# The bias of a spatial gating unit: from a matmul into PSUM to a product on POOL and an add on DVE

## The chip, the cores and the metric

The kernel runs on one core of a Trainium2 chip. The metric is the device time of one execution in microseconds (us); a profile of one execution goes with it. The engines are named as in the profile: PE (matmul), PEld (its weight loads), DVE (vector), ACT (scalar), POOL (GpSimd) and SP (which only issues DMAs here).

## The reference

Grouped attention of 16 query heads over 4 key and value heads, followed by a gated feed-forward unit whose gate mixes the tokens of a sequence. The types are FP32 outside.

```python
# batch 8, 16 q heads, 4 kv heads, seq 384, head_dim 64; d_model 1024, d_ff 1024
k = np.repeat(k, 4, axis=1); v = np.repeat(v, 4, axis=1)
scores = q @ k.transpose(0, 1, 3, 2) / sqrt(64)
attn = softmax(scores)
x = (attn @ v).transpose(0, 2, 1, 3).reshape(8, 384, 1024)

h = np.maximum(x @ w_in, 0.0)
u, v = h[..., :512], h[..., 512:]
v_n = (v - mean(v)) / np.sqrt(var(v) + 1e-06)          # over the 512 features
v_s = einsum('ts,bsd->btd', w_spatial, v_n) + b_spatial[None, :, None]
out = (u * v_s) @ w_out                                # 8 x 384 x 1024
```

The bias belongs to a token t and is the same for all features.

## The kernel before

All matmuls are FP16 with FP32 sums in PSUM. The instruction order of each engine is the order in which the program issues, written out by hand; an engine runs its own list in order and waits on semaphores for the others.

**The outer loop** (L552) counts steps n from 0 to 149, 18 for each batch b (NU = 18). A step issues, in this order:
- what is due by the table `todo`: loads, casts of k, q and v to FP16 on POOL, DMA transposes on SP (`k_turn`, `q_turn`, `x_turn`);
- `scores` (L243): for one group of heads and one key tile a pair of score matmuls into `sc` (L252) and an exp on ACT into `aT` (L259). From batch 1 on, every even step issues two of these and every odd step none;
- `weigh` (L261): 12 matmuls of `aT` against v into the PSUM tile `av` (L266), then on DVE a reciprocal (L276) and the scaling into `x16` (L278, called x in the profile). `av` has one buffer. With rem = n mod 18, a weighing comes at every rem that leaves 0 or 1 when divided by 3, and none where it leaves 2;
- transposes on PE by the table `turns` (batch 0, batch 1 and the end of the last batch);
- `run_fill`: a share of the gated unit of the batch whose attention is finished.

**The gated unit** is a Python generator, `gated_unit` (L306), that yields after each matmul the number of its columns, and `run_fill` (L542) takes from it until the step's share is used up. For a batch it holds 24 matmuls for v (three token tiles of eight, L314, with relu, statistics and their aggregate on DVE, L324 to L327), 32 for u (L336, relu on ACT, L344), the normalisation of v (ACT L346 and L347, DVE `nmr` L349, POOL `vn` L354), 16 for the gating, and 24 for the projection (L384, with copies to `osb` on DVE and ACT in turn, L393, and the stores on SP). Its columns are counted in `COLS`, 43008, and a step takes COLS/18. The unit of batch b starts at n = 18(b+1) + 2, and that of batch 0 earlier, at n = 13, with smaller shares up to n = 20.

**The gating** (L364 to L377) makes, for each of four feature tiles m, one PSUM tile `psp` of 128 features by 384 tokens: first a matmul of the constant `ones_b` against `bias_b` (L366), then three of `vn` against the transposed spatial weights (L369). `ones_b` has ones in rows 0 and 32; `bias_b` holds in row 0 the bias in FP16 and in row 32 what FP16 leaves of it, in the order of the token tiles, so that the matmul adds the bias with nearly FP32 precision. DVE multiplies `psp` by `uT` into `gT` (L377). `prep_spatial` (L408) fills `bias_b` on POOL at step 20, from `b32`, which is loaded at step 13.

Fill tiles share one PSUM tag, `ck`, with three buffers: `pv`, `pu`, `psp` and `po`, and the transposes.

Of the kernel before, what the change touches and what calls it, by code (L numbers as in the profile page):

```python
# [9 lines left out]
FP32 = mybir.dt.float32  # L10
FP16 = mybir.dt.float16
AF = mybir.ActivationFunctionType
ALU = mybir.AluOpType
# [4 lines left out]
def kernel(  # L18
# [28 lines left out]
    scale = D ** -0.5  # L47
    VW = D + 2
    NU = 18
# [235 lines left out]
    def x_tile(b):  # L285
        if b not in xts:
            xts[b] = att.tile([P, NT, NB, P], FP16, name=f"xt_{b}", tag="xt")
        return xts[b]
# [13 lines left out]
        )  # L302

    def gated_unit(b):  # L306
        xt = x_tile(b)
        last = b == B - 1
        mv = small.tile([P, NT, 2], FP32, name=f"mv_{b}", tag="mv")
        v_r, v_n = [], []  # L310
        for st in range(NT):
            pv = ps_ck.tile([P, 512], FP32, name=f"pv_{b}_{st}", tag="ck")
            for kt in range(NB):
                nc.tensor.matmul(  # L314
                    pv,
                    xt[:, st, kt],
                    w_in16[:, kt, DH:DFF],
                    start=(kt == 0),
                    stop=(kt == NB - 1),
                )  # L320
                if kt < NB - 1:
                    yield 512
            vr = moe.tile([P, DH], FP32, name=f"vr_{b}_{st}", tag="vr", bufs=4)
            nc.vector.tensor_scalar(vr, pv, 0.0, None, op0=ALU.max)  # L324
            stats = small.tile([P, 6], FP32, name=f"stats_{b}_{st}", tag="stats")
            nc.vector.bn_stats(stats, vr)  # L326
            nc.vector.bn_aggr(mv[:, st, :], stats)  # L327
            v_r.append(vr)
            yield 512
        rstd = small.tile([P, NT], FP32, name=f"rstd_{b}", tag="rstd")  # L330
        nmr = small.tile([P, NT], FP32, name=f"nmr_{b}", tag="nmr")
        uT = moe.tile([P, NM, S], FP16, name=f"uT_{b}", tag="uT")
        for m in range(NM):
            pu = ps_ck.tile([P, 512], FP32, name=f"pu_{b}_{m}", tag="ck")
            for kt in range(NB):
                nc.tensor.matmul(  # L336
                    pu[:, 0:S].rearrange("p (t s) -> p t s", t=NT),
                    w_in16[:, kt, m * P : (m + 1) * P],
                    xt[:, :, kt],
                    start=(kt == 0),  # L340
                    stop=(kt == NB - 1),
                )
                yield S
            nc.scalar.activation(uT[:, m, :], pu[:, 0:S], AF.Relu)  # L344
            if m == 0:
                nc.scalar.activation(rstd, mv[:, :, 1], AF.Ln, bias=eps_t)  # L346
                nc.scalar.activation(rstd, rstd, AF.Exp, scale=-0.5)  # L347
            if m == 1:
                nc.vector.scalar_tensor_tensor(  # L349
                    nmr, mv[:, :, 0], -1.0, rstd, op0=ALU.mult, op1=ALU.mult  # L350
                )
                for st in range(NT):
                    vn = moe.tile([P, DH], FP16, name=f"vn_{b}_{st}", tag="vn", bufs=6)
                    nc.gpsimd.tensor_scalar(  # L354
                        vn,
                        v_r[st],
                        rstd[:, st : st + 1],
                        nmr[:, st : st + 1],
                        op0=ALU.mult,
                        op1=ALU.add,  # L360
                    )
                    v_n.append(vn)
        gT = moe.tile([P, NM, S], FP16, name=f"gT_{b}", tag="gT")
        for m in range(NM):  # L364
            psp = ps_ck.tile([P, 512], FP32, name=f"psp_{b}_{m}", tag="ck")
            nc.tensor.matmul(psp[:, 0:S], ones_b, bias_b, start=True, stop=False)  # L366
            yield S
            for st in range(NT):
                nc.tensor.matmul(  # L369
                    psp[:, 0:S],  # L370
                    v_n[st][:, m * P : (m + 1) * P],
                    wsT16[:, st, :],
                    start=False,
                    stop=(st == NT - 1),
                )
                yield S
            nc.vector.tensor_tensor(gT[:, m, :], psp[:, 0:S], uT[:, m, :], ALU.mult)  # L377
        rows = out[b].rearrange("(p t) d -> p t d", t=NT)
        for tt in range(NT):
            osb = ops.tile([P, DM], FP32, name=f"osb_{b}_{tt}", tag="osb")  # L380
            for half in range(2):
                po = ps_ck.tile([P, 512], FP32, name=f"po_{b}_{tt}_{half}", tag="ck")
                for m in range(NM):
                    nc.tensor.matmul(  # L384
                        po,
                        gT[:, m, tt * P : (tt + 1) * P],
                        w_out16[:, m, half * 512 : (half + 1) * 512],
                        start=(m == 0),
                        stop=(m == NM - 1),
                    )  # L390
                    yield 512
                cols = slice(half * 512, (half + 1) * 512)
                (nc.scalar.copy if half else nc.vector.tensor_copy)(osb[:, cols], po)  # L393
                if last:
                    nc.sync.dma_start(rows[:, tt, cols], osb[:, cols])
            if not last:
                nc.sync.dma_start(rows[:, tt, :], osb)

    HV = NB * 512
    COLS = NT * HV + NM * NB * S + NM * (NT + 1) * S + NT * 2 * NM * 512  # L400


    b32 = cst.tile([1, S], FP32, name="b32")

    def load_b():
        nc.sync.dma_start(b32, moe_b_spatial.rearrange("(a s) -> a s", a=1))

    def prep_spatial():  # L408
        lo32 = cst.tile([1, S], FP32, name="lo32")
        bp = b32.rearrange("a (p t) -> a t p", t=NT)  # L410
        hi = bias_b[0:1, :].rearrange("a (t p) -> a t p", t=NT)
        nc.gpsimd.tensor_copy(hi, bp)
        nc.gpsimd.tensor_tensor(lo32.rearrange("a (t p) -> a t p", t=NT), bp, hi, ALU.subtract)
        nc.gpsimd.tensor_copy(bias_b[32:33, :], lo32)

    def load_ws():
        t = cst.tile([P, NT, S], FP32, name="ws32")
# [117 lines left out]
            elif m > 3:  # L535
                at(s0 + 3 * m + 5, x_turn, b, 2, 4 * (m - 4), 4 * (m - 3))

    fill = []
    owed = 0.0
    total = NU * B  # L540

    def run_fill(cols):  # L542
        nonlocal owed
        owed = owed + cols if fill else 0.0
        while fill and owed > 0:
            try:
                owed -= next(fill[0])
            except StopIteration:
                fill.pop(0)

    early = 0
    for n in range(total + 6):  # L552
        for f, args in todo.pop(n, []):
            f(*args)
        if n + 1 < NU:
            scores(n + 1)
        elif n >= NU and n % 2 == 0 and n < total:
            scores(n)
            scores(n + 1)
        for hh in range(2):  # L560
            b, r = divmod(n - 3 - hh, NU)
# [4 lines left out]
        if n == 13:  # L566
            fill.append(gated_unit(0))
        if n >= 2 * NU + 2 and (n - 2) % NU == 0 and (n - 2) // NU <= B:
            fill.append(gated_unit((n - 2) // NU - 1))
# [7 lines left out]
    for g in fill:  # L577
        for _ in g:
            pass
    assert not todo and not turns  # L580
# [1 line left out]
_INS = ['q', 'k', 'v', 'moe_w_in', 'moe_w_spatial', 'moe_b_spatial', 'moe_w_out']  # L582
# [26 lines left out]
```

## Time and profile before

| | |
|---|---|
| time, median of 3 runs | 257.72 us (257.62 to 259.6) |
| profiled execution | 256.98 us, of which the span is 254.9 us |
| granted TensorE clock | 0.999 |
| PE busy | 244.5 us (96%) |
| ACT busy | 169.0 us (66%) |
| DVE busy | 140.6 us (55%) |
| POOL busy | 73.8 us (29%) |
| HBM read, written | 25.76 MB, 12.58 MB |

The span runs from the first to the last instruction. Busy time is the union over an engine's instructions; the mean of one instruction can be longer than its share of that, since matmuls overlap. A row of the groups gives line, engine, operation, output from inputs, shapes and count, then busy us and mean ns of one, and the idle time before them with what ended most of it. A row of the timeline gives start and length in us, then engine and operation, with neighbours of one kind merged (x2, x3).

### The profile page before, as it was taken

The numbers are of one execution on the slowest core, as the hardware profiler recorded it, in microseconds if no ns is written. First come the engines' busy times: TensorE is split into PE (matmuls) and PEld (weight loads), VectorE is DVE, ScalarE is ACT, GpSimd is POOL, SyncE is SP. The second block draws the span as 40 slices with busy tenths as digits, with TensorE's granted clock in tenths as the row PEclk, the third lists the DMA queues.
The fourth block names the chain that finished last, engine by engine and source line by source line (L and its number), as shares of the span: only waits on it lengthen the run. The fifth ranks groups of instructions, "written<-read, shape, count | busy, mean of one in ns | idle before, by whom it ended". The sixth has DMA issues, their size and how long they took to land.

```text
span 254.9 us, 5897 instructions
## 1 busy us (share of the span) xinstructions
PE 244.5 (96%) x2400; PEld 126.6 (50%) x2400; DVE 140.6 (55%) x368; ACT 169.0 (66%) x219; POOL 73.8 (29%) x116
## 2 busy tenths in 40 slices
PE   6899899899999999999999999999999999999994
PEld 6565444544455445544455445544455445545551
DVE  2568775364736456454736456454736456465542
ACT  3897566767686767767686767767686767761221
POOL 2446699652032500343032500342030000300210
PEclk9999999999999999999999999999999999999999
DMA  7999899999269971999359991999277364026006
GB/s 184 326 357 346 299 372 326 212 323 299 64 117 302 232 247 25 202 302 281 95 111 293 257 239 30 165 324 346 39 88 152 102 188 41 3 44 247 0 4 245
DMA packets 78828, 49.86 MB, mean 196 GB/s; under 512 B 48081, under 2 KB 72658, under 8 KB 78802
## 3 DMA queue, kind: packets, MB, share of 16 engines
q1 hardware_dynamic: 77762, 49.23, 74.1%
q8 instruction: 19, 0.31, 0.5%
q10 hardware_dynamic: 1040, 0.26, 0.5%
q14 instruction: 7, 0.06, 0.1%
HBM read 25.76 MB, written 12.58 MB: 150 GB/s over the span
## 4 chain that ended last, share of the span: by engine, by line
PE 88%; ACT 3%; DVE 3%; DMA 2%; issue 1%; POOL 1%; SPq 0%; DVEq 0%; POOLq 0%
PE pu L336 16%; PE av L266 16%; PE po L384 15%; PE pv L314 14%; PE sc L252 14%; PE psp L369 6%; PE warm L453 3%; DMA xt<-x 2%; ACT aT L259 2%; PE psp L366 2%; PE qps L217 1%; ACT osb L393 1%; DVE x L278 1%; DVE gT L377 1%; POOL vn L354 1%
## 5 line engine op out<-in xcount | busy, mean ns | idle before, releaser
L259 ACT ACTIVATE aT<-sc 128x1024 f16<-128x1024 f32 x144 | 139.6, 1022 | 56.9 <-PE sc L252 56.5
L266 PEld LDWEIGHTS <-aT 128*128 128x128 f16 x1152 | 44.0, 97 | 30.5 <-issue 6.2
L276 DVE RECIPROCAL r<-av 128x4 f32<-128x4 f32 x96 | 17.0, 177 | 67.2 <-PE av L266 67.2
L266 PE MATMUL av<-v,aT 128*128 128x65 f16 x1152 | 52.3, 194 | 1.1 <-DVE x L278 0.8
L354 POOL TENSOR_SCALAR vn<-vr,rstd,nmr 128x512 f16<-128x512 f32 x24 | 18.2, 774 | 113.4 <-DVE nmr L349 91.7
L336 PE MATMUL pu<-xt,w_in 128*128 128x384 f16 x256 | 47.8, 326 | 0.6 <-ACT uT L344 0.6
L384 PE MATMUL po<-w_out,gT 128*128 128x512 f16 x192 | 47.8, 379 | 0.4 <-ACT osb L393 0.3
L314 PE MATMUL pv<-w_in,xt 128*128 128x512 f16 x192 | 47.2, 379 | 0.6 <-DMA xt<-x 0.4
L252 PE MATMUL sc<-qT,kT 64*128 64x512 f16 x288 | 45.0, 382 | 1.0 <-DVE qT L224 0.6
L278 DVE TENSOR_TENSOR x<-av,r 128x256 f16<-128x256 f32 x96 | 40.7, 424 | 3.3
L336 PEld LDWEIGHTS <-w_in 128*128 128x128 f16 x256 | 23.1, 98 | 15.9 <-issue 3.4
L189 POOL CAST q<-q 128x768 f16<-128x768 f32 (+1 forms) x36 | 25.5, 740 | 18.3 <-DMA q<-in_q_dram 13.6
L314 PEld LDWEIGHTS <-xt 128*128 128x128 f16 x192 | 16.7, 97 | 18.5 <-DMA xt<-x 2.4
L384 PEld LDWEIGHTS <-gT 128*128 128x128 f16 x192 | 16.7, 97 | 16.1 <-DVE gT L377 1.7
L377 DVE TENSOR_TENSOR gT<-psp,uT 128x384 f16<-128x384 f32 x32 | 17.7, 556 | 10.5 <-PE psp L369 9.8
L369 PE MATMUL psp<-wsT,vn 128*128 128x384 f16 x96 | 22.3, 326 | 0.7 <-POOL vn L354 0.7
L252 PEld LDWEIGHTS <-kT 64*128 64x128 f16 x288 | 9.1, 94 | 27.0 <-issue 25.2
L324 DVE TENSOR_SCALAR vr<-pv 128x512 f32<-128x512 f32 x24 | 16.6, 691 | 10.2 <-PE pv L314 9.7
L393 ACT COPY osb<-po 128x512 f32<-128x512 f32 x24 | 14.1, 589 | 12.1 <-PE po L384 12.1
L344 ACT ACTIVATE uT<-pu 128x384 f16<-128x384 f32 x32 | 15.6, 492 | 9.3 <-PE pu L336 9.3
L393 DVE COPY osb<-po 128x512 f32<-128x512 f32 x24 | 16.5, 687 | 6.1 <-PE po L384 6.0
L326 DVE BATCH_NORM_STATS2 stats<-vr 128x6 f32<-128x512 f32 x24 | 16.7, 694 | 0.8
(48 smaller groups left out, 113.5 us busy)
## 6 DMA issues: line engine op xcount, KB each, us to landing
q<-in_q_dram SPq DMA_DIRECT2D x14, 768.0 KB, 7.5
out_dram<-osb SPq DMA_DIRECT2D x21, 512.0 KB, 3.6
wi<-in_moe_w_in_dram SPq DMA_DIRECT2D x4, 1024.0 KB, 8.8
v<-in_v_dram SPq DMA_DIRECT2D x8, 384.0 KB, 8.6
k<-in_k_dram SPq DMA_DIRECT2D x7, 384.0 KB, 4.6
wo<-in_moe_w_out_dram SPq DMA_DIRECT2D x2, 1024.0 KB, 5.9
out_dram<-osb SPq DMA_DIRECT2D x6, 256.0 KB, 2.1
q<-in_q_dram SPq DMA_DIRECT2D x2, 512.0 KB, 7.2
```

Of the source, the lines that this page charges most:

```text
L189: f(q16s[b, j][:, lo:hi, :, hh, :], src[:, hh, lo:hi])
L252: nc.tensor.matmul(sc[:, hh], kTs[b][half, j, t * P : (t + 1) * P], qTs[b, j][half, qt], start=True, stop=True,)
L259: nc.scalar.activation(aTs[b, m][:, t], sc, AF.Exp, scale=scale)
L266: nc.tensor.matmul(av[:, i, :], aTs[b, m][:, t, hh, i * P : (i + 1) * P], v1[b % 2][:, 2 * j + hh, t, 0 : D + 1], start=(t == 0), stop=(t ...
L278: nc.vector.tensor_tensor(x16s[b][:, qt, blk : blk + 2].rearrange("p k (i d) -> p (k i) d", i=2), av[:, :, 0:D], r.to_broadcast([P, G, D]) ...
L314: nc.tensor.matmul(pv, xt[:, st, kt], w_in16[:, kt, DH:DFF], start=(kt == 0), stop=(kt == NB - 1),)
L336: nc.tensor.matmul(pu[:, 0:S].rearrange("p (t s) -> p t s", t=NT), w_in16[:, kt, m * P : (m + 1) * P], xt[:, :, kt], start=(kt == 0), stop ...
L354: nc.gpsimd.tensor_scalar(vn, v_r[st], rstd[:, st : st + 1], nmr[:, st : st + 1], op0=ALU.mult, op1=ALU.add,)
L369: nc.tensor.matmul(psp[:, 0:S], v_n[st][:, m * P : (m + 1) * P], wsT16[:, st, :], start=False, stop=(st == NT - 1),)
L377: nc.vector.tensor_tensor(gT[:, m, :], psp[:, 0:S], uT[:, m, :], ALU.mult)
L384: nc.tensor.matmul(po, gT[:, m, tt * P : (tt + 1) * P], w_out16[:, m, half * 512 : (half + 1) * 512], start=(m == 0), stop=(m == NM - 1),)
L393: (nc.scalar.copy if half else nc.vector.tensor_copy)(osb[:, cols], po)
```

## The change

The matmul against `ones_b` goes, and with it `ones_b` and the two-row form of `bias_b`. `bias_b` becomes a 128-partition FP32 tile; the DMA that loads `b32` broadcasts the bias to all partitions, and `prep_spatial` is one POOL copy that sorts it into the order of the token tiles.

The output of a gate is now written as u*psp + u*bias. POOL makes the second term, `ub`, one FP32 product of 128 x 384 for each m (`biases`, issued after the four blocks of u). DVE makes the first term into an FP32 tile `g` and adds `ub` into `gT`: two DVE operations for each m where there was one.

The generator is cut into pieces that one endless `stream` puts in order. In it, v of the next batch's first token tile stands between the gating and the projection of a batch, so a batch's own part starts with its second token tile. The normalisation is issued after the first block of u instead of partly after the second. `COLS` loses the bias matmuls (41472), the small shares of the start last one step longer (up to n = 21), and from n = 22 the stream goes on with COLS/18 for each step from n = 40, so that batch b's own part starts at n = 18(b+1) + 4 for b of 1 and above. `osb` has three buffers instead of four.

```diff
-    ops = ctx.enter_context(tc.tile_pool(name="ops", bufs=4))
+    ops = ctx.enter_context(tc.tile_pool(name="ops", bufs=3))
...
-    ones_b = cst.tile([P, P], FP16, name="ones_b")
-    nc.gpsimd.memset(ones_b, 0.0)
-    nc.gpsimd.memset(ones_b[0:1, :], 1.0)
-    nc.gpsimd.memset(ones_b[32:33, :], 1.0)
-    bias_b = cst.tile([P, S], FP16, name="bias_b")
-    nc.gpsimd.memset(bias_b, 0.0)
+    bias_b = cst.tile([P, S], FP32, name="bias_b")
...
+    def biases(b):
         for m in range(NM):
+            nc.gpsimd.tensor_tensor(ubs[b][:, m, :], uTs[b][:, m, :], bias_b, ALU.mult)
...
+    def gate(b, m):
...
-            nc.tensor.matmul(psp[:, 0:S], ones_b, bias_b, start=True, stop=False)
-            yield S
...
-            nc.vector.tensor_tensor(gT[:, m, :], psp[:, 0:S], uT[:, m, :], ALU.mult)
+        g = moe.tile([P, S], FP32, name=f"g_{b}_{m}", tag="g")
+        nc.vector.tensor_tensor(g, psp[:, 0:S], uTs[b][:, m, :], ALU.mult)
+        nc.vector.tensor_tensor(gTs[b][:, m, :], g, ubs[b][:, m, :], ALU.add)
+        yield S
...
+    def stream():
+
+        yield from v_tile(0, 0)
+        for b in range(B):
+            yield from v_tile(b, 1)
+            yield from v_tile(b, 2)
+            for m in range(NM):
+                yield from u_block(b, m)
+                if m == 0:
+                    normal(b)
+            biases(b)
+            for m in range(NM):
+                yield from gate(b, m)
+            if b + 1 < B:
+                yield from v_tile(b + 1, 0)
+            for tt in range(NT):
+                yield from project(b, tt)
...
-    COLS = NT * HV + NM * NB * S + NM * (NT + 1) * S + NT * 2 * NM * 512
+    COLS = NT * HV + NM * NB * S + NM * NT * S + NT * 2 * NM * 512
...
-        if n < NU + 3:
-            if 13 <= n and early < 2 * HV:
+        if n < NU + 4:
+            if n >= 13 and early < 2 * HV:
...
-            run_fill((COLS - (early if n < 2 * NU + 2 else 0)) / (NU if n >= 2 * NU + 2 else NU - 1))
+            run_fill((COLS + (HV - early if n < 2 * NU + 4 else 0)) / NU)
```

More of the change, by code (lines that the diff above doesn't have):

```diff
@@ L302, in x_turn @@
         )
[L306 to L329, printed above, removed]
+    mvs, v_rs, v_ns, uTs, ubs, gTs = {}, {}, {}, {}, {}, {}
@@ new lines, in v_tile @@
+    def v_tile(b, st):
+        if st == 0:
+            mvs[b] = small.tile([P, NT, 2], FP32, name=f"mv_{b}", tag="mv")
+            v_rs[b] = []
+        pv = ps_ck.tile([P, 512], FP32, name=f"pv_{b}_{st}", tag="ck")
+        for kt in range(NB):
+            nc.tensor.matmul(
+                pv,
+                x_tile(b)[:, st, kt],
+                w_in16[:, kt, DH:DFF],
+                start=(kt == 0),
+                stop=(kt == NB - 1),
+            )
+            if kt < NB - 1:
+                yield 512
+        vr = moe.tile([P, DH], FP32, name=f"vr_{b}_{st}", tag="vr", bufs=4)
+        nc.vector.tensor_scalar(vr, pv, 0.0, None, op0=ALU.max)
+        stats = small.tile([P, 6], FP32, name=f"stats_{b}_{st}", tag="stats")
+        nc.vector.bn_stats(stats, vr)
+        nc.vector.bn_aggr(mvs[b][:, st, :], stats)
+        v_rs[b].append(vr)
+        yield 512
@@ L330, in gated_unit, with normal @@
+    def normal(b):
         rstd = small.tile([P, NT], FP32, name=f"rstd_{b}", tag="rstd")
         nmr = small.tile([P, NT], FP32, name=f"nmr_{b}", tag="nmr")
-        uT = moe.tile([P, NM, S], FP16, name=f"uT_{b}", tag="uT")
-        for m in range(NM):
-            pu = ps_ck.tile([P, 512], FP32, name=f"pu_{b}_{m}", tag="ck")
-            for kt in range(NB):
-                nc.tensor.matmul(
[L337 to L341, printed above, removed]
-                )
-                yield S
[L344 to L390, printed above, removed]
-                    yield 512
[L392 to L397, printed above, removed]
+        nc.scalar.activation(rstd, mvs[b][:, :, 1], AF.Ln, bias=eps_t)
@@ new lines, in normal @@
+        nc.scalar.activation(rstd, rstd, AF.Exp, scale=-0.5)
+        nc.vector.scalar_tensor_tensor(
+            nmr, mvs[b][:, :, 0], -1.0, rstd, op0=ALU.mult, op1=ALU.mult
+        )
+        v_ns[b] = []
+        for st in range(NT):
+            vn = moe.tile([P, DH], FP16, name=f"vn_{b}_{st}", tag="vn", bufs=6)
+            nc.gpsimd.tensor_scalar(
+                vn,
+                v_rs[b][st],
+                rstd[:, st : st + 1],
+                nmr[:, st : st + 1],
+                op0=ALU.mult,
+                op1=ALU.add,
+            )
+            v_ns[b].append(vn)
@@ new lines, in u_block @@
+    def u_block(b, m):
+        if m == 0:
+            uTs[b] = moe.tile([P, NM, S], FP16, name=f"uT_{b}", tag="uT")
+            ubs[b] = moe.tile([P, NM, S], FP32, name=f"ub_{b}", tag="ub", bufs=1)
+        pu = ps_ck.tile([P, 512], FP32, name=f"pu_{b}_{m}", tag="ck")
+        for kt in range(NB):
+            nc.tensor.matmul(
+                pu[:, 0:S].rearrange("p (t s) -> p t s", t=NT),
+                w_in16[:, kt, m * P : (m + 1) * P],
+                x_tile(b)[:, :, kt],
+                start=(kt == 0),
+                stop=(kt == NB - 1),
+            )
+            if kt < NB - 1:
+                yield S
+        nc.scalar.activation(uTs[b][:, m, :], pu[:, 0:S], AF.Relu)
+        yield S
@@ new lines, in biases @@
+    def biases(b):
+        for m in range(NM):
+            nc.gpsimd.tensor_tensor(ubs[b][:, m, :], uTs[b][:, m, :], bias_b, ALU.mult)
+    def gate(b, m):
+        if m == 0:
+            gTs[b] = moe.tile([P, NM, S], FP16, name=f"gT_{b}", tag="gT")
+        psp = ps_ck.tile([P, 512], FP32, name=f"psp_{b}_{m}", tag="ck")
+        for st in range(NT):
+            nc.tensor.matmul(
+                psp[:, 0:S],
+                v_ns[b][st][:, m * P : (m + 1) * P],
+                wsT16[:, st, :],
+                start=(st == 0),
+                stop=(st == NT - 1),
+            )
+            if st < NT - 1:
+                yield S
+        g = moe.tile([P, S], FP32, name=f"g_{b}_{m}", tag="g")
+        nc.vector.tensor_tensor(g, psp[:, 0:S], uTs[b][:, m, :], ALU.mult)
+        nc.vector.tensor_tensor(gTs[b][:, m, :], g, ubs[b][:, m, :], ALU.add)
+        yield S
@@ new lines, in project @@
+    def project(b, tt):
+        last = b == B - 1
+        rows = out[b].rearrange("(p t) d -> p t d", t=NT)
+        osb = ops.tile([P, DM], FP32, name=f"osb_{b}_{tt}", tag="osb")
+        for half in range(2):
+            po = ps_ck.tile([P, 512], FP32, name=f"po_{b}_{tt}_{half}", tag="ck")
+            for m in range(NM):
+                nc.tensor.matmul(
+                    po,
+                    gTs[b][:, m, tt * P : (tt + 1) * P],
+                    w_out16[:, m, half * 512 : (half + 1) * 512],
+                    start=(m == 0),
+                    stop=(m == NM - 1),
+                )
+                if m < NM - 1:
+                    yield 512
+            cols = slice(half * 512, (half + 1) * 512)
+            (nc.scalar.copy if half else nc.vector.tensor_copy)(osb[:, cols], po)
+            if last:
+                nc.sync.dma_start(rows[:, tt, cols], osb[:, cols])
+            if half == 0:
+                yield 512
+        if not last:
+            nc.sync.dma_start(rows[:, tt, :], osb)
+        yield 512
@@ new lines, in stream @@
+    def stream():
[5 more added lines that the diff above has]
+                yield from u_block(b, m)
+                if m == 0:
+                    normal(b)
+            biases(b)
+            for m in range(NM):
+                yield from gate(b, m)
[3 more added lines that the diff above has]
+                yield from project(b, tt)
@@ L399 @@
     HV = NB * 512
-    COLS = NT * HV + NM * NB * S + NM * (NT + 1) * S + NT * 2 * NM * 512
-    b32 = cst.tile([1, S], FP32, name="b32")
+    COLS = NT * HV + NM * NB * S + NM * NT * S + NT * 2 * NM * 512
+    b32 = cst.tile([P, S], FP32, name="b32")
     def load_b():
-        nc.sync.dma_start(b32, moe_b_spatial.rearrange("(a s) -> a s", a=1))
+        nc.sync.dma_start(b32, moe_b_spatial.rearrange("(a s) -> a s", a=1).to_broadcast([P, S]))
     def prep_spatial():
[L409 to L414, printed above, removed]
+        nc.gpsimd.tensor_copy(
+            bias_b.rearrange("q (t p) -> q t p", t=NT), b32.rearrange("q (p t) -> q t p", t=NT)
+        )
@@ L536 @@
                 at(s0 + 3 * m + 5, x_turn, b, 2, 4 * (m - 4), 4 * (m - 3))
-    fill = []
+    fill = stream()
     owed = 0.0
@@ L543, in run_fill @@
         nonlocal owed
[L544 to L549, printed above, removed]
+        owed += cols
+        while owed > 0:
+            owed -= next(fill, 1e9)
     early = 0
@@ L565 @@
             f(*args)
[L566 to L569, printed above, removed]
-        if n < NU + 3:
-            if 13 <= n and early < 2 * HV:
+        if n < NU + 4:
+            if n >= 13 and early < 2 * HV:
                 c = min(768, 2 * HV - early)
@@ L575 @@
         else:
-            run_fill((COLS - (early if n < 2 * NU + 2 else 0)) / (NU if n >= 2 * NU + 2 else NU - 1))
-    for g in fill:
-        for _ in g:
-            pass
+            run_fill((COLS + (HV - early if n < 2 * NU + 4 else 0)) / NU)
+    for _ in fill:
+        pass
     assert not todo and not turns
```

## The prediction

> **What bounds it now.** I read the page's shares first, then busy time by stretch, then groups by form, then the timeline of one gating and of the tail.
>
> ```profile
> PE 244.5 (96%) x2400; PEld 126.6 (50%) x2400; DVE 140.6 (55%) x368; ACT 169.0 (66%) x219; POOL 73.8 (29%) x116
> 146.60:175.10 28.50, 28.50 (x279) 14.15 (x280) 15.97 (x42) 20.69 (x27) 7.29 (x11) 1.00 0.85 205
> 232.00:254.90 22.90, 18.91 (x101) 9.48 (x99) 10.11 (x20) 4.81 (x10) 2.28 (x3) 0.99 0.28 107
> ```
>
> Columns of the stretches: length, then busy us of PE, PEld, DVE, ACT, POOL. In a whole batch (28.5 us) PE has no gap: a matmul less is time less, and a PE stall is time more. DVE's 56% there is an average, so it says nothing yet on a burst. The tail, where the last batch runs alone, has gaps.
>
> ```profile
> L366 PE MATMUL psp<-bias_b,ones_b 128*128 128x384 f16 x32 | 10.4, 325 | 0.0
> L377 DVE TENSOR_TENSOR gT<-psp,uT 128x384 f16<-128x384 f32 x32 | 17.7, 556 | 10.5 <-PE psp L369 9.8
> L278 DVE TENSOR_TENSOR x<-av,r 128x256 f16<-128x256 f32 x96 | 40.7, 424 | 3.3
> L413 POOL TENSOR_TENSOR lo<-b,bias_b 1x384 f32<-1x384 f32 x1 | 1.0, 1012 | 0.1
> ```
>
> **Removed: 32 bias matmuls.** Their 325 ns overlap: three queued 384-wide ones take 0.65 us, the last 0.33 of it, so the pitch is 0.162. 28 of them lie in gapless stretches: 28 x 0.162 = -4.5 us. The last four belong to the tail.
>
> **Added on DVE: 32 adds behind the gating.** No row has a sum of two FP32 SBUF operands. Ends: 0.35 us (the 128x384 copy of kT, L212) and 0.69 (the 512-wide statistics from SBUF, L326). L278 and L377 give (556-424)/128 = 1.03 ns an element plus 0.16 us, both two-input TENSOR_TENSOR; I take 0.556. Where they queue decides:
>
> ```profile
> 193.51 0.42 DVE L278 TENSOR_TENSOR x<-av,r 128x256 f16<-128x256 f32 x1
> 193.85 0.56 DVE L377 TENSOR_TENSOR gT<-psp,uT 128x384 f16<-128x384 f32 x1
> ...
> 195.78 0.54 PE L266 MATMUL av<-v,aT 128*128 128x65 f16 x12
> ...
> 196.36 0.18 DVE L276 RECIPROCAL r<-av 128x4 f32<-128x4 f32 x1
> ...
> 196.57 0.42 DVE L278 TENSOR_TENSOR x<-av,r 128x256 f16<-128x256 f32 x1
> ...
> 197.87 0.51 PE L266 MATMUL av<-v,aT 128*128 128x65 f16 x11
> ```
>
> av has one PSUM buffer. The av at 197.87 may start only when DVE's reciprocal and x behind the av of 195.78 are done (196.99): 0.88 us to spare. The gating's DVE work is issued ahead of that reciprocal. Count in steps n of the outer loop, rem = n mod 18, with zero at the sc of rem 12 (190.82). New fill per step is 41472/18 = 2304 columns, starting at n = 40 for batch 1; walking the generator through gives: rem 12: u x5, gate 0 x1; rem 13: x2, x3, x1 of gates 0, 1, 2; rem 14: x2, x3 of gates 2, 3 and one v; rem 15: five v; rem 16: two v, two po. Each of rem 12 to 15 holds as many columns as before, so the second av still wants to start at 197.87-190.82 = 7.05.
>
> DVE: x of rem 13 starts at 2.69 (193.51). A next independent instruction follows 0.34 later (193.85), that is 0.08 before the end; a dependent one some 0.04 after (nmr, reciprocal to x). First gating product 3.03 (rem 13's fill starts at 193.09, so at 2.27; psp's last matmul, the second there, starts 2.43 and ends 2.76), its add 3.62 to 4.18, and a pair every 1.07: last add 6.83 to 7.39, reciprocal 7.31, x 7.52 to 7.95, av 8.0. Stall 8.0-7.05 = 0.95 us, for 7 batches +6.65. With adds of 0.35 it is 0.15; with 0.69, 1.5. What is late next (v statistics, osb copy) catches up within three steps, as rem 14 and 17 have no weighing.
>
> **Added on POOL: 32 products.** Ends: 0.48 us (half of the pair of 128x384 k casts, 0.96) and 1.23 (two passes of the 512-wide cast, L134). I take 1.0 by L413, the one two-input operation there with 384 elements. POOL has room, but:
>
> ```profile
> 42.28 1.60 POOL L189 CAST q<-q 128x768 f16<-128x768 f32 x2
> 42.49 0.63 DVE L349 SCALAR_TENSOR_TENSOR nmr<-mv,rstd 128x3 f32<-128x3 f32 x1
> ...
> L349 DVE SCALAR_TENSOR_TENSOR nmr<-mv,rstd x8: 160/162/626, 42.5 to 240.4; 128x3 f32<-128x3 f32 x8
> ```
>
> This DVE operation with two SBUF inputs takes 0.16 us, but 0.63 where a POOL cast is under way: it ends at 43.12, as the first of two casts of 0.8 ends. The new add is of that kind. The first three products of a batch run ahead while u is made. The fourth waits for uT's last part (relu behind the two exps, done 2.76 as at 193.58 now) and holds 2.8 to 3.8, so the first add waits 0.15: +1.05 over 7 batches. In batches 0 to 4, POOL's casts for three batches on fall here too:
>
> ```profile
> 137.08 0.96 POOL L173 CAST k<-k 128x384 f16<-128x384 f32 x2 [3.59 <-DMA k<-in_k_dram]
> 139.60 1.60 POOL L189 CAST q<-q 128x768 f16<-128x768 f32 x2 [1.57 <-DMA q<-in_q_dram]
> ```
>
> With that batch's sc at 133.77 they lie at 3.3 to 4.3 and 5.8 to 7.4. If adds and casts take turns, three adds wait 0.45, 0.33 and 0.33 us: 1.1 at most, 0 if they miss; I take 0.4: +2.0 for five batches.
>
> [...]
>
> **Tail.** No weighing is left; what counts is the last gT.
>
> ```profile
> 243.20 0.65 PE L369 MATMUL psp<-wsT,vn 128*128 128x384 f16 x3
> ...
> 244.61 1.86 DVE L377 TENSOR_TENSOR gT<-psp,uT 128x384 f16<-128x384 f32 x3 [0.16 <-PE psp L369]
> ...
> 246.52 1.41 PEld L384 LDWEIGHTS <-gT 128*128 128x128 f16 x8 [0.55 <-DVE gT L377]
> ```
>
> From the end of vn (243.04) to the last gT: 3.4 us. Now the first product can start 0.69 in; without exclusion the pairs end at 0.69+0.59+0.56+3x1.07 = 5.05: +1.6. But POOL makes the four ub from 0 to 4, only then being free of vn. Taking turns, adds run 2.0, 3.56, 5.12 and, POOL then empty, 6.19 to 6.74: +3.3. If POOL goes first all along, 7.8: +4.4. I take 3.3. The cover between gating and projection isn't there for the last batch.
>
> **Moved.** v's first tile goes between gating and projection; its matmuls, DVE and DMA work stay the same in number. Its x transpose (SP, rem 8) is 7 steps old then. Projection and its stores come some 2.4 steps later: on SP the store of rem 18 stands before the x transpose of rem 20 and waits for osb some 1 us; v's third tile wants that transpose at rem 23.8, near 6 us on, before 3.4 steps. So nothing is lost, and the waits of v on xt (0.4 us of PE idle) may go. POOL's 2.2 us of bias preparation shrink to one copy, which may end PE's 0.7 us wait for vn in batch 0. Together -1.1 (0 if POOL's inputs bound it). Three osb buffers are as many as a batch uses; the broadcast load of b (196 KB) is 0.6 us at the 322 GB/s of that stretch, off the chain.
>
> **Sum.** -4.5 +6.65 +1.05 +2.0 +3.3 -1.1 = +7.4. The profiled execution took 256.98 (span 254.9 and 2.1 around it): 264.3. The median of the runs, 257.72, lies 0.7 higher.
>
> **Rivals.**
> 1. *PE's saving stands* (17%): DVE's order absorbs the adds, no stall. 256.98-4.5+1.6-1.1 = 253.0. For it: PE 100% busy, DVE 56%. Against: the count above. It decides once an add costs under some 0.28 us (then the pairs end 1.1 us sooner); with a tail of 3.3 the sign turns at a stall of 0.33 a batch.
> 2. *Queue without exclusion* (18%): products of 0.48 or misses. 256.98-4.5+6.65+1.6-1.1 = 259.6. For it: nmr is one tiny instance. Against: it ends with the cast.
> 3. *POOL wins each turn* (15%): casts cost 1.1 in five batches and the tail 4.4: 264.3+3.5+1.1 = 268.9.
> My forecast has 50%.
>
> 1% (2.6 us) is about what this measurement can tell. Rival 1 gives faster, rival 2 within 1% (255.1 to 260.3), the others slower: 0.16, 0.19, 0.65 with a little for the edges. Range 255 to 269, leaving out most of rival 1 and the far end of 3; the likeliest case alone: 261 to 267.
>
> **What would show it.** PE idle before L266 waiting for DVE x, some 1 us once a batch; adds longer than 0.56 where POOL is busy; POOL products near 1.0; a batch period of 29 us instead of 28.5; the last gT some 6.7 us after vn. A period of 27.9 without a wait of av on x would prove me wrong.

## The result and the profile after

The changed kernel takes 271.39 us (median of 4 runs, 269.66 to 273.07) against 257.67 us for the kernel before in the same comparison: a ratio of 1.0515, with a 95% interval of 1.0432 to 1.0599. The profiled execution took 271.25 us, of which 269.5 us is the span. The forecast was 264.3 us: the sign is right and the loss about half the real one (+7.4 forecast, +14.3 between the two profiled executions, +14.6 in the span). Some executions run at a lower clock and take longer (w2: 274.46 us at 0.981, 268.07 at 1.00); the ratios here, and the medians given for x2 and w2, leave those out.

The first line of the page after, then four of its groups (out<-in, shapes, count, busy us, mean ns of one, idle before and its releaser), and last the row of `av` from the page before:

```profile
PE 244.9 (91%) x2368; PEld 123.8 (46%) x2368; DVE 157.0 (58%) x400; ACT 171.0 (63%) x219; POOL 106.0 (39%) x142
...
L261 PE MATMUL av<-v,aT 128*128 128x65 f16 x1152 | 53.4, 194 | 13.2 <-DVE x L273 12.7
...
L395 PE MATMUL po<-w_out,gT 128*128 128x512 f16 x192 | 49.5, 390 | 2.4 <-DVE gT L385 1.9
...
L367 POOL TENSOR_TENSOR ub<-uT,bias_b 128x384 f32<-128x384 f16 x32 | 29.6, 949 | 5.0 <-ACT uT L362 5.0
...
L385 DVE TENSOR_TENSOR gT<-g,ub 128x384 f16<-128x384 f32 x32 | 20.0, 625 | 4.1 <-DVE g L384 0.5
...
L266 PE MATMUL av<-v,aT 128*128 128x65 f16 x1152 | 52.3, 194 | 1.1 <-DVE x L278 0.8
```

PE has 32 matmuls less, but its busy time is what it was (244.9 us against 244.5), while the span is 14.6 us longer: its share falls from 96% to 91%, and nearly all of the difference is idle time. The largest wait stands in the second line: av waits 12.7 us for x, against 0.8 before. POOL's products take 0.949 us (taken: 1.0) and the adds 0.625 on the mean (taken: 0.556 and turns).

**Where the 14.6 us lie.** Cut at the score pair that opens each gating (rem 12), the two traces differ by -1.0 us up to step 30, +2.9 in the batch from step 30 to 48, +7.4 in the five batches from 48 to 138, +1.4 from there to the first psp of the last batch (25.14 against 23.75), and +3.9 from that psp to the end (15.77 against 11.86). So it is not one event. The last whole batch took 28.47 us before and 29.86 after; the two stretches, before and after (length, then busy us of PE, PEld, DVE, ACT, POOL, then granted clock):

```profile
190.82:219.29 28.47, 28.47 (x277) 14.12 (x278) 15.95 (x41) 20.70 (x27) 2.28 (x3) 1.00 0.52 110
198.73:228.59 29.86, 28.32 (x273) 13.62 (x274) 17.55 (x45) 20.99 (x28) 5.85 (x8) 1.00 0.36 89
```

PE is idle 1.54 us of the second, where it had no gap before. The timeline of the gating shows the larger part, DVE's row and the av it holds up:

```profile
201.77 0.55 DVE L384 TENSOR_TENSOR g<-psp,uT 128x384 f32<-128x384 f32 x1
202.42 0.56 DVE L385 TENSOR_TENSOR gT<-g,ub 128x384 f16<-128x384 f32 x1
202.90 0.55 DVE L384 TENSOR_TENSOR g<-psp,uT 128x384 f32<-128x384 f32 x1
...
205.81 0.56 DVE L385 TENSOR_TENSOR gT<-g,ub 128x384 f16<-128x384 f32 x1
206.29 0.17 DVE L271 RECIPROCAL r<-av 128x4 f32<-128x4 f32 x1
206.50 0.42 DVE L273 TENSOR_TENSOR x<-av,r 128x256 f16<-128x256 f32 x1
...
206.98 0.54 PE L261 MATMUL av<-v,aT 128*128 128x65 f16 x12 [1.11 <-DVE x L273]
```

Four pairs lie ahead of the reciprocal that frees `av`, and PE stands 1.11 us. A second wait, of 0.40 us, comes some 10 us earlier, where nothing of the gating runs:

```profile
195.30 0.20 ACT L329 ACTIVATE rstd<-rstd 128x3 f32<-128x3 f32 x1
195.54 0.16 DVE L330 SCALAR_TENSOR_TENSOR nmr<-mv,rstd 128x3 f32<-128x3 f32 x1 [1.83 <-ACT rstd L329]
195.62 0.18 DVE L271 RECIPROCAL r<-av 128x4 f32<-128x4 f32 x1
...
196.31 0.54 PE L261 MATMUL av<-v,aT 128*128 128x65 f16 x12 [0.40 <-DVE x L273]
```

This is the normalisation, which the change issues behind the first block of u. `nmr` sits at the head of DVE's list and waits 1.83 us for ACT's rstd, which stands behind two exps and a relu; the reciprocal behind it waits too, though its own input is there.

The tail, POOL, DVE and PE:

```profile
253.62 4.17 POOL L367 TENSOR_TENSOR ub<-uT,bias_b 128x384 f32<-128x384 f16 x4
255.08 0.74 DVE L385 TENSOR_TENSOR gT<-g,ub 128x384 f16<-128x384 f32 x1
...
258.77 0.56 DVE L385 TENSOR_TENSOR gT<-g,ub 128x384 f16<-128x384 f32 x1
259.39 6.39 PE L395 MATMUL po<-w_out,gT 128*128 128x512 f16 x21 [0.74 <-DVE gT L385]
```

The last gT is ready at 259.33, 5.7 us after vn (253.65), where it was 3.4 before. But the 21 matmuls that follow take 6.39 us. PE alone by stretch, with the granted clock as the number behind the count:

```profile
250.00:255.90 5.90, 5.84 (x36) 1.00 0.00 0
255.90:259.40 3.50, 1.17 (x4) 1.00 0.00 0
259.40:263.10 3.70, 3.70 (x10) 0.54 0.20 77
263.10:266.00 2.90, 2.68 (x13) 1.00 0.62 232
```

After 3.5 us in which PE worked a third of the time, the next 3.7 us run at a clock of 0.54: eight matmuls at a pitch of 0.43 us instead of 0.216, +1.7 us.

### The profile page after: what moved, and what is told of

The parts are those of the page before. It is cut to its first block, busy times and chain, and to the rows that moved or that the text cites. A ratio compares the mean times of both kernels' runs of the same rounds, so it can differ in the third digit from the quotient of the medians.

```text
span 269.5 us, 5907 instructions
## 1 busy us (share of the span) xinstructions
PE 244.9 (91%) x2368; PEld 123.8 (46%) x2368; DVE 157.0 (58%) x400; ACT 171.0 (63%) x219; POOL 106.0 (39%) x142
## 4 chain that ended last, share of the span: by engine, by line
PE 60%; DVE 17%; issue 9%; ACT 5%; DMA 4%; POOL 2%; SPq 1%; DVEq 0%; POOLq 0%
PE po L395 15%; PE av L261 13%; PE pv L308 10%; PE pu L353 9%; PE sc L247 9%; DVE g L384 6%; DMA q<-in_q_dram 4%; DVE x L273 4%; DVE gT L385 3%; PE warm L483 3%; ACT aT L254 2%; DVE r L271 1%; ACT uT L362 1%; POOL vn L336 1%; PE qps L212 1%
## 5 line engine op out<-in xcount | busy, mean ns | idle before, releaser
L261 PE MATMUL av<-v,aT 128*128 128x65 f16 x1152 | 53.4, 194 | 13.2 <-DVE x L273 12.7
L395 PE MATMUL po<-w_out,gT 128*128 128x512 f16 x192 | 49.5, 390 | 2.4 <-DVE gT L385 1.9
L308 PE MATMUL pv<-w_in,xt 128*128 128x512 f16 x192 | 50.5, 378 | 0.6 <-DVE g L384 0.6
L184 POOL CAST q<-q 128x768 f16<-128x768 f32 (+1 forms) x36 | 29.4, 849 | 6.7 <-DMA q<-in_q_dram 6.6
L367 POOL TENSOR_TENSOR ub<-uT,bias_b 128x384 f32<-128x384 f16 x32 | 29.6, 949 | 5.0 <-ACT uT L362 5.0
L385 DVE TENSOR_TENSOR gT<-g,ub 128x384 f16<-128x384 f32 x32 | 20.0, 625 | 4.1 <-DVE g L384 0.5
L362 ACT ACTIVATE uT<-pu 128x384 f16<-128x384 f32 x32 | 15.8, 495 | 9.4 <-PE pu L353 9.3
L374 PE MATMUL psp<-wsT,vn 128*128 128x384 f16 x96 | 19.6, 327 | 0.5 <-POOL vn L336 0.4
```

The lines of the kernel that those rows point to most:

```text
L184: f(q16s[b, j][:, lo:hi, :, hh, :], src[:, hh, lo:hi])
L261: nc.tensor.matmul(av[:, i, :], aTs[b, m][:, t, hh, i * P : (i + 1) * P], v1[b % 2][:, 2 * j + hh, t, 0 : D + 1], start=(t == 0), stop=(t ...
L308: nc.tensor.matmul(pv, x_tile(b)[:, st, kt], w_in16[:, kt, DH:DFF], start=(kt == 0), stop=(kt == NB - 1),)
L367: nc.gpsimd.tensor_tensor(ubs[b][:, m, :], uTs[b][:, m, :], bias_b, ALU.mult)
L385: nc.vector.tensor_tensor(gTs[b][:, m, :], g, ubs[b][:, m, :], ALU.add)
L395: nc.tensor.matmul(po, gTs[b][:, m, tt * P : (tt + 1) * P], w_out16[:, m, half * 512 : (half + 1) * 512], start=(m == 0), stop=(m == NM - 1),)
```

## The experiments

All ratios are to the kernel before, with the 95% interval. "Batch" is the time from one score pair of rem 12 to the next, late in the run, where POOL has no more casts (28.47 before, 29.86 after). It is much sharper than the total: within most profiles, batches of one kind agree to some 0.1 us (in x3 and y4 those with casts differ by 0.6 and 1.6), while totals spread over 1 to 6 us.

| kernel | median us | ratio [95%] | batch |
|---|---|---|---|
| after | 271.39 | 1.0515 [1.0432, 1.0599] | 29.86 |
| x1 no add | 256.79 | 0.9949 [0.9913, 0.9985] | 28.69 |
| x2 nmr later | 269.69 | 1.0447 [1.0368, 1.0526] | 29.51 |
| x3 one product | 268.46 | 1.0411 [1.0333, 1.0490] | 29.65 |
| x4 tail cover | 270.54 | 1.0495 [1.0417, 1.0574] | 29.86 |
| y1 no bias | 252.09 | 0.9776 [0.9705, 0.9848] | 27.79 |
| y2 move only | 259.12 | 1.0013 [0.9971, 1.0055] | 28.73 |
| y3 late adds | 265.55 | 1.0285 [1.0191, 1.0380] | 28.68 |
| y4 late adds, nmr later | 265.98 | 1.0312 [1.0239, 1.0385] | 28.22 |
| z3 last by matmul | 268.38 | 1.0383 [1.0325, 1.0441] | 29.9, the last 31.34 |
| y5 = y4, last by matmul | 263.79 | 1.0208 [1.0145, 1.0270] | 28.22 |
| z1 = y5, adds on POOL | 256.17 | 0.9921 [0.9891, 0.9950] | 28.41 |
| z2 = y5, loads later | 255.12 | 0.9887 [0.9838, 0.9936] | 28.22 |
| w1 = z2, copies swapped | 253.93 | 0.9802 [0.9756, 0.9848] | 28.05 |
| w2 = after, loads later | 269.65 | 1.0397 [1.0329, 1.0465] | 29.86 |

**x1, the add alone left out.** The output lacks u*bias; POOL still makes the products.

```diff
-        nc.vector.tensor_tensor(g, psp[:, 0:S], uTs[b][:, m, :], ALU.mult)
-        nc.vector.tensor_tensor(gTs[b][:, m, :], g, ubs[b][:, m, :], ALU.add)
+        nc.vector.tensor_tensor(gTs[b][:, m, :], psp[:, 0:S], uTs[b][:, m, :], ALU.mult)
```

> The changed kernel without the add on DVE: its gating writes psp times uT straight into gT, as before the change; the products of u and bias are still made on POOL but nothing reads them, so the bias is left out. Theory Q (the adds queue ahead of the reciprocal that frees av): the wait of 1.2 us before the second weighing behind the gating goes in all seven batches (8.3 us), and the tail gives back 2.3 us of waiting and 1.7 us of matmuls at half rate: 271.4 - 12 = 259. Theory M (it is the new order, with the normalisation earlier and the projection later): the waits there stay and the time is above 265.

256.79 us, the first of the two readings. DVE in the same place:

```profile
195.80 1.05 DVE L383 TENSOR_TENSOR gT<-psp,uT 128x384 f16<-128x384 f32 x2 [0.44 <-PE psp L374]
196.81 0.18 DVE L271 RECIPROCAL r<-av 128x4 f32<-128x4 f32 x1
```

DVE now waits for psp instead of running behind it. A batch falls from 29.86 to 28.69: the adds in their place cost 1.17 us a batch, and with the tail (15.77 to 11.25, from the first psp of the last batch to the end) they are most of the loss. Yet x1, which has neither bias matmuls nor adds, saves only 0.5% on the kernel before. The -4.5 of the sum isn't there either.

**x2, nmr and vn issued behind the second block of u.**

```diff
             for m in range(NM):
                 yield from u_block(b, m)
                 if m == 0:
                     normal(b)
+                if m == 1:
+                    normal_v(b)
```

`normal` keeps Ln and Exp on ACT; `normal_v` holds nmr on DVE and vn on POOL.

> The changed kernel with nmr and vn issued behind the second block of u again, Ln and Exp of rstd staying behind the first. Theory N: nmr on DVE waits 1.83 us for ACT, whose list has two exps ahead of it, and holds the reciprocal behind it: 0.46 us of PE a batch, so 271.4 - 6 x 0.46 = 268.6, and no wait of av on x is left ahead of the gating. Rival: what is gained there is lost again at the stall behind the gating, as products and adds come later too: 271.4, no change.

The total, 269.69, is not to be told from after's by its interval, but the batch is 29.51 instead of 29.86, and in steps without gating av no longer waits. The wait of `nmr` costs 0.35 us a batch.

**x3, POOL's products made for batch 0 alone** (the other batches add that batch's term).

```diff
-            ubs[b] = moe.tile([P, NM, S], FP32, name=f"ub_{b}", tag="ub", bufs=1)
+            ubs[b] = ubs[0] if b else moe.tile([P, NM, S], FP32, name=f"ub_{b}", tag="ub", bufs=1)
...
-            biases(b)
+            if b == 0:
+                biases(b)
```

> The changed kernel with POOL's products made in batch 0 alone and read by all adds, so that the bias term of the other batches is that of batch 0 (left out: their own products). Theory Q: only POOL's hold on the adds goes, 0.1 to 0.2 us a batch and some 0.6 us in the tail: 269 to 270.5. Theory L (it is the exclusion between DVE's two-input adds and POOL's products): 6 us or more come back, 265 or less.

268.46 us, 29.65 a batch. The queue of adds costs almost as much without POOL's products, so it is DVE's order, not POOL's share of the work, that makes most of the stall; the rival that blamed POOL's products falls. Of the 2.9 us that the total gains, 2.3 lie in the profile's tail.

**x4, PE kept busy in the tail's gap** with 16 matmuls into a spare PSUM tile.

```diff
+                if b == B - 1:
+                    cover = ps_sc.tile([P, 2, 512], FP32, name="cover", tag="sc")
+                    for _ in range(16):
+                        nc.tensor.matmul(cover[:, 0], ident16, w_out16[:, 0, 0:512], start=True, stop=True)
```

> The changed kernel with 16 matmuls of 512 columns, whose result nobody reads, between gating and projection of the last batch, where PE otherwise waits 3.5 us for the last gT. Theory C (the projection's first matmuls run at a pitch of 0.43 us instead of 0.216 because PE had idled): the pitch is 0.216 from the first one, the granted clock 1.0, 271.4 - 1.7 = 269.7, and the runs lie closer together. Rival: the slow matmuls wait for something else (gT, PSUM, stores): 271.4 and the pitch stays 0.43.

PE's rows:

```profile
255.83 3.62 PE L432 MATMUL cover<-w_out,ident 128*128 128x512 f16 x16
259.28 5.34 PE L395 MATMUL po<-w_out,gT 128*128 128x512 f16 x24
```

24 projection matmuls in 5.34 us, a pitch of 0.216. From the first psp to the last copy on ACT it is 10.78 us instead of 12.09. In the total (270.54) the 1.3 us drown. Nor does one profile show that the cover prevents the drop. y3 below keeps after's tail, and in its profile a gap of the same length (3.56 us with three matmuls in it, against 3.55) is followed by full speed:

```profile
254.79 4.71 PE L403 MATMUL po<-w_out,gT 128*128 128x512 f16 x21 [0.74 <-DVE gT L372]
```

x3's gap of 3.0 us is also followed by 4.71 us; y4's of 3.55 us by 6.39, as in after. So the drop doesn't always come.

**y1, the kernel before without its bias matmuls** (the bias is left out, and its columns are taken out of `COLS`).

```diff
-            nc.tensor.matmul(psp[:, 0:S], ones_b, bias_b, start=True, stop=False)
-            yield S
```

> The kernel before without the 32 bias matmuls and with their columns taken out of the step's share; nothing else is changed, so the bias is left out. If PE bounds it as read, 28 x 0.162 us go from the gapless stretches and up to 0.65 from the tail: 257.7 - 4.5 to 5.2 = 252.5 to 253.2. Rival: another engine takes over and less than half of that comes.

252.09 us, a ratio of 0.9776, a batch 0.68 less than before (4 x 0.17) and a span of 249.9, 5.0 less. The first term of the sum is right, in the order of before.

**y2, the change's order with the old arithmetic** (bias matmul, one DVE product, no products on POOL).

```diff
+        nc.tensor.matmul(psp[:, 0:S], ones_b, bias_b, start=True, stop=False)
+        yield S
...
-        nc.vector.tensor_tensor(g, psp[:, 0:S], uTs[b][:, m, :], ALU.mult)
-        nc.vector.tensor_tensor(gTs[b][:, m, :], g, ubs[b][:, m, :], ALU.add)
+        nc.vector.tensor_tensor(gTs[b][:, m, :], psp[:, 0:S], uTs[b][:, m, :], ALU.mult)
...
-            biases(b)
```

> The order of the changed kernel (v's next tile between gating and projection, normalisation behind the first block of u, the later start) with the bias matmuls of before and no product and no add. Theory Q with N: the move alone costs nmr's wait, 0.46 us in 6 batches, and 0.2 us a batch where an exp now stands behind an osb copy on ACT: 257.7 + 2.8 + 1.3 - 1 = 260.8. As predicted at first: 257.7 - 1.1 = 256.6.

The total says nothing (1.0013, with 1 inside the interval). The batch is 28.73 against 28.47: the order, with its three `osb` buffers, costs 0.26 us a batch. And beside x1 (28.69) the bias matmuls, worth 0.68 in the old order, are worth 0.04 in the new one. PE's time by what it starts, from each start to the next, in the same batch:

| | before | y1 | y2 | x1 | after | y4 | w1 |
|---|---|---|---|---|---|---|---|
| psp | 2.74 | 2.04 | 2.71 | 2.05 | 2.11 | 2.06 | 2.05 |
| sc, with the waits of the av behind it | 4.85 | 4.86 | 5.16 | 5.30 | 6.50 | 4.86 | 4.86 |
| av | 4.56 | 4.56 | 4.56 | 4.82 | 4.78 | 4.79 | 4.63 |
| pv | 5.38 | 5.38 | 5.45 | 5.63 | 5.56 | 5.56 | 5.58 |
| whole batch | 28.47 | 27.79 | 28.73 | 28.69 | 29.86 | 28.22 | 28.05 |

From y2 to x1 psp gives back 0.66, and `sc`, `av` and `pv` take 0.14, 0.26 and 0.18. x1 also has POOL's products, which y2 lacks; but x3, without them in this batch, has nearly the same av and pv (4.79 and 5.63), so they don't stretch these. Nor is it the third `osb` buffer: no copy in y2, x1 or after waits for a store. What remains is likely that with fewer columns the step's share is shorter, and the waits and copies lie otherwise against the exps; this was not isolated. What stretches av is in after's timeline:

```profile
212.88 0.59 ACT L405 COPY osb<-po 128x512 f32<-128x512 f32 x1 [0.58 <-PE po L395]
213.36 1.95 ACT L254 ACTIVATE aT<-sc 128x1024 f16<-128x1024 f32 x2
...
214.19 0.75 PE L261 MATMUL av<-v,aT 128*128 128x65 f16 x12
```

A projection copy stands on ACT ahead of two exps; the av that uses them takes 0.75 us instead of 0.54.

**y3, the adds issued inside v's first tile of the next batch**, two at its fourth matmul and two at its sixth, with the `g` of each m kept in one tile of the batch. The last batch keeps its order.

```diff
-                yield from v_tile(b + 1, 0)
+                for i, cols in enumerate(v_tile(b + 1, 0)):
+                    if i in (3, 5):
+                        add(b, i - 3)
+                        add(b, i - 2)
+                    yield cols
```

> The changed kernel with the same adds, issued two at a time behind the fourth and the sixth matmul of the next batch's v tile, so behind the next reciprocal instead of ahead of it; the four products g of a batch have a tile of their own in the staging buffers of the weights. The last batch keeps its order. Theory Q: the order on DVE is the whole of the 1.2 us, so 271.4 - 7 x 1.2 = 263, with the adds no cheaper. Rival: DVE is simply too full there, the wait moves to the next weighing or to the projection: above 268.

265.55 us, between the two. In the last whole batch the period is 28.68, x1's: the stall of the adds is gone whole. In the batches with casts it stays at 29.5 to 29.9: there the adds are late, and PE waits 0.3 to 0.7 us for gT at the projection.

**y4, y3 and x2 together**: the edits of both diffs above.

> The two together, late adds and nmr behind the second block of u. If both waits are separate their gains add: 271.4 - 8.4 - 2.8 = 260.2, of which the tail still costs 4 us against before. If they overlap: 263.

265.98 us, far over what was expected, and the reason is clear from two batches of its own trace. The last row is from a batch without casts, the others from one with them:

```profile
82.27 1.61 POOL L184 CAST q<-q 128x768 f16<-128x768 f32 x2
82.72 4.22 DVE L378 TENSOR_TENSOR gT<-g,ub 128x384 f16<-128x384 f32 x4
84.53 2.01 POOL L184 CAST q<-q 128x768 f16<-128x768 f32 x2 [0.65 <-DMA q<-in_q_dram]
...
87.00 1.04 PE L409 MATMUL po<-w_out,gT 128*128 128x512 f16 x4 [0.71 <-DVE gT L378]
...
203.75 1.96 DVE L378 TENSOR_TENSOR gT<-g,ub 128x384 f16<-128x384 f32 x4
```

The same four adds take 1.96 us alone and 4.22 beside POOL's q casts, and PE's projection waits for them. Of the four, the one that starts while POOL is idle takes 0.55 us, the others 1.57, 1.17 and 1.17, and the cast between the last two takes 1.15 instead of 0.8: the two engines hold each other up, as if they took turns. The last batch, without casts, takes 28.22, two of those with them 30.5, and the others 29.2 and 30.8.

**z3, after with its last batch's bias by the old matmul**, no product and no add there.

```diff
+        last = b == B - 1
+        if last:
+            nc.tensor.matmul(psp[:, 0:S], ones_b, bias_r, start=True, stop=False)
+            yield S
...
+        if last:
+            nc.vector.tensor_tensor(gTs[b][:, m, :], psp[:, 0:S], uTs[b][:, m, :], ALU.mult)
+            yield S
+            return
```

> The changed kernel, but the last batch takes its bias by the matmul of before (no product and no add there; osb has two buffers, to make room for both forms of the bias). Theory T: the tail's loss is the late last gT, 2.3 us, and the half-rate matmuls behind that wait, 1.3 to 1.7 us: 271.4 - 3.8 = 267.6, projection at a pitch of 0.216 throughout. Rival: the tail is longer for what was moved into it: less than 2 us come back.

268.38 us. From the first psp of the last batch to the end it is 12.0 us instead of 15.8, at full clock:

```profile
257.92 5.59 PE L409 MATMUL po<-w_out,gT 128*128 128x512 f16 x24
```

The tail's 3.8 us come back as expected, but z3's last whole batch takes 31.34, where those ahead of it take 29.94. z3 has two `osb` buffers, and in four batches one of DVE's copies into osb waits 2.1 us for a store, which no copy of after does. In the long batch a copy starts 3.63 us late, at 217.14, the reciprocal and x stand behind it, and PE's av waits for x:

```profile
218.43 0.54 PE L267 MATMUL av<-v,aT 128*128 128x65 f16 x12 [1.41 <-DVE x L279]
```

That is the 1.4 us. The profile names no store as the cause of this one wait, so that the missing buffer made it is likely and not shown.

**y5, y4 with that diff**, but with three `osb` buffers.

> Late adds and nmr behind the second block of u, with the last batch by the bias matmul. Against the same kernel without the last step (265.98) theory T gives -3.8: 262.2. What is left over the kernel before is the exclusion of adds and POOL casts in batches 0 to 4, some 2 us in each of three or four of them.

263.79 us, 2.2 less than y4 (a ratio of 1.0208 against 1.0312): less than the 3.8 that z3's tail gave back. In the profiles the tail gives back all of it (11.87 us against 15.72), but y5's is 3.1 us behind y4's at step 48, with a granted clock of 0.89 between 47 and 63 us where y4's has 1.00. Whether that holds for the other runs was not followed.

**z1, y5 with the adds on POOL**, behind the gating.

```diff
-        nc.vector.tensor_tensor(gTs[b][:, m, :], gs[b][:, m, 0:S], ubs[b][:, m, :], ALU.add)
+        nc.gpsimd.tensor_tensor(gTs[b][:, m, :], gs[b][:, m, 0:S], ubs[b][:, m, :], ALU.add)
```

> As the run before it, but POOL makes the adds too, in its own list behind the four products; DVE has no operation with two SBUF inputs in the gating any more. Theory E (what is left is the exclusion between two-input adds and POOL's casts): every batch takes the 28.2 us that the batches without casts showed, against 28.47 before, so 262.2 - 4 x 2 = 254 to 256, under the kernel before. Rival P: POOL's adds at 0.95 us each come too late for the projection: PE waits for gT, above 259.

256.17 us, and every later batch 28.41, with casts or without. POOL's adds are nearly twice as long as DVE's (1.002 us against 0.551 in z2 below), and a batch takes 0.19 us more than y5's 28.22; in one engine's list adds and casts follow one another, and neither is beside the other:

```profile
L384 POOL TENSOR_TENSOR gT<-g,ub 128x384 f16<-128x384 f32 x28 | 27.1, 1002 | 0.0
```

**z2, y5 with the next loads of k, q and v issued four steps later**, so that the casts miss the adds.

```diff
-                at(w0 - NU + 11, load_k, b)
+                at(w0 - NU + 15, load_k, b)
```

(and the same for q and v)

> Late adds on DVE, nmr behind the second block of u, last batch by matmul, and the loads of k, q and v for the batch after next issued four steps later, so that POOL's casts of them fall behind the gating. Theory E: the adds are back at 0.56 us and all batches take 28.2 us: 254 to 256. Rival: it is not the casts; or the loads now hold up the transposes of x on SP's queue: no better than 262.

255.12 us. The adds are short everywhere, and the later batches run at 28.22 (one of them 28.57):

```profile
L384 DVE TENSOR_TENSOR gT<-g,ub 128x384 f16<-128x384 f32 x28 | 13.7, 551 | 0.0
```

Four steps of the loads are worth 8.7 us here (263.79 to 255.12): the second way to take the collision away.

**w1, z2 with the copies of the second token tile swapped** between ACT and DVE, so that no copy stands ahead of the two exps.

```diff
-            (nc.scalar.copy if half else nc.vector.tensor_copy)(osb[:, cols], po)
+            (nc.scalar.copy if half != (tt == 1) else nc.vector.tensor_copy)(osb[:, cols], po)
```

> The kernel with late adds, nmr behind the second block of u, last batch by matmul and later loads (255.1, 28.22 us a batch), in which the two copies of the projection's second token tile change engines: its first half by ACT, its second by DVE. Theory A (what the moved order still costs is an osb copy on ACT that stands ahead of the exp that a weighing waits for): the weighing at rem 3 takes 0.54 us instead of 0.75, a batch 28.0, the kernel 253.7. Rival: another copy takes its place, or the DVE copy holds the next reciprocal: no change or worse.

```profile
201.62 0.69 DVE L431 COPY osb<-po 128x512 f32<-128x512 f32 x1 [0.44 <-PE po L421]
201.94 1.94 ACT L260 ACTIVATE aT<-sc 128x1024 f16<-128x1024 f32 x2 [0.47 <-PE sc L253]
...
202.92 0.59 PE L267 MATMUL av<-v,aT 128*128 128x65 f16 x12
```

The copy is on DVE, the exps wait only for their scores, and av takes 0.59. A batch is 28.05, and 253.93 us the best time found: 0.9802 [0.9756, 0.9848] of the kernel before.

**w2, after with the loads later**, to see the casts' price in after itself.

> The changed kernel with nothing but the loads of k, q and v for the batch after next four steps later. Tells what the casts on POOL cost there: by the prediction's term 2.0 us (0.4 in each of five batches), by its upper bound 5.5, by the profile of the change, where four of six batches take 29.9 us with casts or without, 1 to 1.5: 270. The mean of the adds falls from 0.625 towards 0.58 us, while av still waits 1.2 us for x in each batch.

The totals, 269.65 against 271.39, don't differ clearly by their intervals. The batches from step 48 on, at a granted clock of 1.00 in both profiles, are sharper.

```profile
L385 DVE TENSOR_TENSOR gT<-g,ub 128x384 f16<-128x384 f32 x32 | 20.4, 638 | 4.0 <-POOL ub L367 0.5 <-DVE g L384 0.5
```

The adds are no shorter (0.638 against 0.625), and the batches go from some 29.94 to 29.86; only the longest, 30.74, falls to 30.21. In after the casts hardly meet the adds.

## Why the prediction was right or wrong

**Bias matmuls, -4.5: right for before's order, not for the new one.** y1 has it (5.0 of span, with the tail's four). But x1 against y2 shows 0.04 us a batch: the sum took this term and the move as independent, and they are not.

**The queue of adds, 6.65 + 1.05: right.** The count put the first product 3.03 us after the scores of rem 12, x at 7.67 (with the 0.15), and a stall of 1.10; measured were 3.04, 7.77 and 1.11, and 1.17 a batch in the ladder from x1 to after. That y3 removes all of it by the order alone, and x3 hardly any by taking POOL's products away, shows that it is the order. The products' part is the 0.21 us a batch that x3 gains. Its parts were less exact: the wait for the fourth product was under 0.1 rather than 0.15, and the pairs came every 1.13 us, not 1.07.

**The casts, +2.0: too high.** Adds do lengthen beside casts, and dearly where they meet (y4: 4.22 us for four adds instead of 1.96). In after the casts hardly meet the adds, and w2 finds 0.1 us a batch, and 0.5 in one: some 0.9 in all.

**The failed step: the move at no cost.** The prediction weighed the moved transposes, stores and buffers, found that "nothing is lost", and gave the move no cost per batch, only the gain of -1.1 at the start. The runs show 0.90 us a batch in its place (x1's 28.69 against y1's 27.79, both without bias matmuls and adds), an estimated 6.3 us in seven batches; the loss in the span exceeds the forecast by 7.2. With the bias matmuls in place the same order costs 0.26 (y2), so most of the 0.90 comes only when both are done. Two parts of it have a place in the traces.

**The normalisation's new place: no term at all.** The text on the change has it, the prediction doesn't mention it. It did not ask when ACT's list comes to rstd, nor who stands behind `nmr` on DVE. It costs 0.35 (x2) to 0.44 us a batch (sc in x1 against y1), some 2.5 to 3 us in seven batches.

**The moved projection.** It follows the v tile now, so its copies come at other steps, and one lands ahead of two exps. With x1, av and pv take 0.26 and 0.25 us more than in y1. w1 takes back 0.17 of the first, so that part is the copy's. Why pv, which comes in one piece more, takes longer was not settled. Seven times 0.5 is an estimate of another 3.5 us.

**Steady batches together**: -0.68 (y1) +0.90 (the order, x1) +1.17 (the adds) = +1.39, which is 29.86 - 28.47. The prediction had -0.65 + 1.10, and 0.4 where there are casts; the 0.90 is what it lacked.

**The tail, +3.3: +3.9, with two wrong halves.** The last gT came 5.7 us after vn, not 6.7: beside POOL's products the adds took 0.74, 0.62, 0.61 and 0.56 us, less than a whole wait for each product. The other half was not foreseen: in this execution the gap that the adds leave on PE was followed by a lower clock (0.54), +1.7. That 2.3 and 1.7 come near the 3.3 is luck.

**The head, -1.1: -1.0** up to step 30, and the waits of v on xt are gone. But the gating of batch 0 loses 2.9 us, some 1.5 more than a later batch. There psp waits 0.42 us for vn, and av 1.39 for x. What makes the rest was not tried.

**The rivals.** That PE's saving stands (253.0) fails on its condition: DVE's order does not absorb the adds. w1 comes to 253.93 with five edits that take waits away, but by other terms: a batch of 28.05 where y1 has 27.79, and the bias matmul kept in the last batch. The rival without exclusion had products of 0.48 us, which take 0.949, "or misses": y4's two groups of adds speak against the first reading, and w2 shows that in after the casts do mostly miss. Its 259.6 is low for the same step as the forecast, the move. The third, that POOL wins each turn (268.9), comes nearest in time and for a wrong reason: neither casts nor tail cost what it said.

## What to carry to other kernels

An engine's list is a queue, as `nmr` showed with its wait of 1.83 us at the head of DVE's: price each instruction that an edit inserts or moves by the wait at its head and by what stands behind it, here the reciprocal that frees PE's only buffer, and not by its duration. A full engine's saved work was worth its time only where the order around it kept; measure the removal alone and in the new order, since the two differed here by 0.68 against 0.04 us a batch. When totals spread by 1%, cut the trace at an instruction that recurs and compare periods.

## What the runs showed of the hardware that was not expected

**The granted clock in the tail.** After 3.5 us with 1.17 us of PE work, after's PE ran at 0.54 for 3.7 us; with the gap filled (x4) it stayed at 1.00. y3's gap of the same length had no such effect (21 matmuls in 4.71 us behind it, where after's took 6.39). What decides whether the drop comes was not shown. The four runs of after gave 269.66 us at a clock of 1.00, 271.25 and 271.53 at 0.994, and 273.07 at 0.981.

**DVE's adds beside POOL's casts.** Four adds of two SBUF inputs took 4.22 us beside q casts and 1.96 without (y4), 1.06 us each against 0.55 (z2's mean). In after's tail the adds grew by 0.18 us at most beside the products (0.74 us against 0.56), less than a wait for a whole product (0.949 us). Why they grow was not shown.
